# Layer 2's first pass activated by halves of tokens, and a reciprocal issued ahead of its neighbour

## The chip, the cores and the metric

The kernel runs on one core of a Trainium2 chip. The metric is the device time of one execution in microseconds (us): the median of three runs. A core has five engines that run beside each other, each with its own queue worked off in order: TensorE (PE in the profile, with its weight loads as PEld), VectorE (DVE), ScalarE (ACT), GpSimd (POOL) and SyncE (SP), which here only issues DMAs. They wait for each other through semaphores.

## The reference

Attention over 4 batches of 8 heads, 576 tokens, head size 64, with a softmax that keeps only the scores within tau of the maximum, and behind it two feed-forward layers over all 2304 tokens (512 to 2048 to 512). What matters here:

```python
scores = np.where(scores >= thresh, scores, -1000000000.0)
attn = np.exp(scores - np.max(scores, axis=-1, keepdims=True))
attn = attn / (np.sum(attn, axis=-1, keepdims=True) + 1e-09)
x = attn @ v                               # then layer 1, another activation
h = x @ w_in                               # layer 2
r = np.maximum(h, 0.0)
out = (s * (r * r) + b) @ w_out
```

## The kernel before

Every piece of work is a task with a priority, the tiles that it reads and writes, and one or more engines that could do it, with an assumed duration for each. A planner (`Sched.run`) plays the tasks through against these durations and writes the instructions out in the order in which it started them; on the chip each engine then follows that fixed order. Until 460 us of its own clock the planner multiplies the duration of each ACT, DVE and POOL task by a factor between 1.0 and 1.1, taken from a random sequence in the order in which the tasks start:

```python
                    if now < DRAW_TO and e in ("act", "dve", "pool"):
                        t.fn = (e, t.fn[1] * (1.0 + SPREAD * rnd.random()), *t.fn[2:])
```

Attention comes first, in 80 tiles of queries (`qtiles`). 64 of them hold two heads, 16 hold one. A tile goes through the scores on PE, the row minimum (L646, DVE), the exponential (L649, ACT), the mask with its sum (L654, DVE), then three small steps on that sum: `un`, a fallback for empty rows (L667 on POOL or L668 on DVE), `rc`, the sum plus 1e-9 (L670 on POOL or L671 on DVE), and the reciprocal of `rc` (L673, DVE). The normalization (L684 POOL, L689 ACT, or DVE) reads both `rc` and `un`, and PE transposes its result (L715) for the product with the values (L773). `un` and `rc` depend on the same sums and not on each other. Both have the same priority, so the one that is added first goes first.

Matmuls of layer 1 (L968, L1001) have a lower priority than attention and fill PE beside it, once their weights are converted; until 200 us of its clock the planner puts in small matmuls on the identity (L1572, "fills") where PE would otherwise have nothing to do. After attention comes the rest of layer 1, then three passes over the tokens in three blocks of 768: pass 0 is layer 1's second half of the hidden units, pass 1 is layer 2's first half, pass 2 (the last) layer 2's second half. In these passes the order of PE's products is fixed: each product task writes "pe order".

One block of a pass is `gemm1`, seven products p in the order 1, 5, 6, 3, 2, 7, 4 (pass 2: 1, 2, 5, 6, 3, 7, 4), each for four tiles j of hidden units and for n = 384 tokens, and then a second product: `gemm2` with six tiles of tokens over eight rows of hidden units in pass 1 (L1467), `gemm2_products` in pass 2 (L1425). A product's 384 columns in PSUM are copied (`copied`, L1193 ACT or L1194 DVE) or added (`joined`, L1197 DVE) into rows of 768 tokens, `even` and `odd`. `even` has both its halves after p = 3 and p = 2, `odd` after p = 7 and p = 4.

In pass 1 `activated` works on a whole row of 768: positive part (L1229), square (L1230), scale and bias (L1231 DVE, L1232 ACT or L1233 POOL), and a split into a high part (L877, ACT) and a low part (L570 POOL or L571 DVE) that the second product reads. In pass 2 `activated_part` does the first three by halves of 384 (L1243, L1246, L1247 to L1249), and for p = 4 it takes the positive part straight from PSUM (L1245), so that product is not copied. PSUM has eight banks. The products p = 1, 6, 7 and 4 of one j add up in one bank, so four banks stay taken until p = 4 has been read out. The copies and additions have priority -2, ahead of the activations at -1.

Of the kernel before, what the change touches and what calls it, by code (L numbers as in the profile page):

```python
# [12 lines left out]
ALU = mybir.AluOpType  # L13
AX = mybir.AxisListType

B, H, S, D = 4, 8, 576, 64
# [51 lines left out]
BT = 768  # L68
# [308 lines left out]
def attention_then_ffn(tc, qk, v, tau, w1, w2, s2, b2, out):  # L377
    nc = tc.nc
    sch = Sched()

    def add(alts, prio, r=(), w=(), group=None, lag=0, after=0.0):
        mems = {k[0] for k in (*r, *w) if isinstance(k, tuple)}
        r = list(r)
        if "late" not in r and mems & {"LG", "MD"}:
            r.append("late")
        if mems & {"PR", "PF"}:
            r.append("final")
        return sch.add(alts, prio, r, w, group, lag, after)
# [9 lines left out]
    ident = lp.tile([128, 128], F32, name="ident")  # L398
    tau_c, cst = lp.tile([128, 1], F32, name="tau"), lp.tile([128, 5], F32, name="cst")
    half, s_c, b_c, part_c, tiny_c = (cst[:, i:i + 1] for i in range(5))  # L400
# [213 lines left out]
    def qtiles(u, blk):  # L614

        n = ctr["tile"]
        ctr["tile"] += 1
        mixed = blk == 4
        turned = mixed and units[u][0] >= SPLIT
        nx = 1 if mixed else 2  # L620
        p, st = P[n % NP], ST[n % NST]
        kp = [("P", n % NP, x) for x in range(4)]
        ks = [("ST", n % NST, x) for x in range(2)]
        ksm = [("SM", n % NST, x) for x in range(2)]
        krc, kun = ("RC", n % NST), ("UN", n % NST)
        nm, nthr, sm, rc, un = (st[:, 2 * j:2 * j + nx] for j in range(5))
        prs = []
        kth = [("thr", n % NST, x) for x in range(2)]

        def thr(xs, pr):  # L630
            a, o = nm[:, xs[0]:xs[-1] + 1], nthr[:, xs[0]:xs[-1] + 1]
            add([("pool", 300, lambda: nc.gpsimd.tensor_scalar(out=o, in0=a, scalar1=tau_c, scalar2=0.0, op0=ALU.add, op1=ALU.add)),
                 ("dve", 122, lambda: nc.vector.tensor_scalar(out=o, in0=a, scalar1=tau_c, scalar2=None, op0=ALU.add))],
                (-1,) + pr, r=[ks[x] for x in xs] + ["tau"], w=[kth[x] for x in xs])

        def head(x):
            pr = prio_a()
            prs.append(pr)
            ke = kp if mixed else kp[2 * x:2 * x + 2]
            g = scores(u, blk, x)  # L640
            kg = ("bank", g)

            def Sv():
                return PS[g.banks[0]][:, :, 0:HS]

            add([("dve", 665, lambda: nc.vector.tensor_reduce(out=nm[:, x:x + 1], in_=Sv(), axis=AX.XY, op=ALU.min))],  # L646
                at(pr, "min"), r=[kg], w=[ks[x]], group=g)
            ev = p[:, x * S:x * S + S].rearrange("p (a c) -> p a c", a=2)
            add([("act", 624, lambda: nc.scalar.activation(out=ev, in_=Sv(), func=AF.Exp, bias=nm[:, x:x + 1], scale=-1.0))],  # L649
                at(pr, "exp"), r=[kg, ks[x]], w=ke, group=g)  # L650
            thr((x,), pr)

            def mask():
                nc.vector.scalar_tensor_tensor(out=ev, in0=Sv(), scalar=nthr[:, x:x + 1],  # L654
                                               in1=ev, op0=ALU.is_le, op1=ALU.mult, accum_out=sm[:, x:x + 1])

            def late_mask():
                add([("dve", 735, mask)], at(pr, "mask"), r=[kg, kth[x]], w=[ksm[x]] + ke, group=g)

            return late_mask  # L660

        for x in range(nx):
            head(x)()
        pr = prs[-1]

        rs = [ksm[x] for x in range(nx)]
        add([("pool", 240, lambda: nc.gpsimd.tensor_scalar(out=un, in0=sm, scalar1=0.5, scalar2=1.0 / S, op0=ALU.is_lt, op1=ALU.mult)),  # L667
             ("dve", 122, lambda: nc.vector.tensor_scalar(out=un, in0=sm, scalar1=half, scalar2=part_c, op0=ALU.is_lt, op1=ALU.mult))],  # L668
            (-1,) + pr, r=rs + ["ident"], w=[kun])
        add([("pool", 195, lambda: nc.gpsimd.tensor_scalar(out=rc, in0=sm, scalar1=1e-9, scalar2=1.0, op0=ALU.add, op1=ALU.mult)),  # L670
             ("dve", 122, lambda: nc.vector.tensor_scalar(out=rc, in0=sm, scalar1=tiny_c, scalar2=None, op0=ALU.add))],  # L671
            (-1,) + pr, r=rs + ["ident"], w=[krc])
        add([("dve", 75, lambda: nc.vector.reciprocal(out=rc, in_=rc))], (-1,) + pr, w=[krc])  # L673

        def norm(x):
            runs = [(0, 128, x * S, x * S, S)]
            if turned:

                runs = [(64, 128, 0, S, 64), (64, 128, 64, 0, 512), (0, 64, 0, 0, S)]

            def scaled(eng):
                def fn():
                    for i, j, a, o, w in runs:
                        eng.tensor_scalar(out=p[i:j, o:o + w], in0=p[i:j, a:a + w], scalar1=rc[i:j, x:x + 1], scalar2=un[i:j, x:x + 1], op0=ALU.mult, op1=ALU.add)  # L684
                return fn

            def scaled_act():
                for i, j, a, o, w in runs:
                    nc.scalar.activation(out=p[i:j, o:o + w], in_=p[i:j, a:a + w], func=AF.Identity, scale=rc[i:j, x:x + 1], bias=un[i:j, x:x + 1])  # L689

            add([("pool", 2170 if turned else 800, scaled(nc.gpsimd)), ("dve", 1050 if turned else 490, scaled(nc.vector), True),
                 ("act", 2060 if turned else 760, scaled_act)],
                at(pr, "norm"), r=[krc, kun], w=kp if mixed else kp[2 * x:2 * x + 2])

        for x in range(nx):
            norm(x)
        for x in range(nx):
            blocks_of_keys(u, pr, p, kp[3 * x], 0 if not x else S + 64, x, mixed, blk)
        if mixed:
            last_keys(u, pr, p, kp[1:3], mixed, blk, kp[:1])  # L700
        else:
            tails.append((p, kp[1:3]))
            if blk % 2:
                two_tails(u, pr, blk)
# [559 lines left out]
    def gemm1(P, T, first):  # L1264
# [17 lines left out]
        for p in P.order:  # L1282
            pe, sp, po = fresh()
            i = P.order.index(p)
            if p == 4:
                P.early = pe[1] - 1
            r = first_ring[i] if first else ring[i % len(ring)]
            for o, u, v in made.get(p, ()):
                add(both_tt(T, o[0], u[0], v[0], ALU.subtract), sp, r=u[1] + v[1], w=o[1])
            split(T, lambda r=r: r(0, T), lambda r=r: r(BT, T), val[p][0], val[p][1], r.keys(0, T), r.keys(BT, T), sp, pairs_of)  # L1290
            for j in range(nj):
                if p == 1:
                    A[j] = Group(ANY if first else ANY8)
                elif p == 5:
                    Bk[j] = Group(ANY8)
                g = A[j] if p in (1, 6, 7, 4) else Bk[j] if p in (5, 3) else Group(ANY8)
                u = P.unit[P.product(p, j)]

                def mm(g=g, u=u, r=r, p=p):
                    o = bank[g.banks[0]][:, 0:n]  # L1300
                    i = 0
                    for k in range(2):
                        ah, al = u(k * 128, 128), u(256 + k * 128, 128)
                        xh, xl = r(k * n, n), r(BT + k * n, n)
                        for a, y in ((ah, xh), (ah, xl), (al, xh)):
                            nc.tensor.matmul(o, a, y, start=(i == 0 and p in (1, 5, 2)), stop=(i == 5), skip_group_check=p not in (1, 5, 2))  # L1306
                            i += 1

                product(pe, 6 * mm_ns(n), mm, u.keys() + r.keys() + ["four"] * (first and p == ORDER[1]), g)
                even, odd = even_b[j], odd_b[j]  # L1310
                row, at_, n_ = {1: (even, 0, 0), 5: (odd, n, 0), 6: (even, n, 0), 3: (even, n, 1), 7: (odd, n, 1), 2: (even, 0, 1), 4: (odd, 0, 0)}[p]
                whole = P.last and p == 4
                if not whole:
                    (joined if n_ else copied)(g, n, lambda row=row, at_=at_: row(at_, n), row.keys(at_, n), po)
                if P.last:
                    if p in (3, 2, 7, 4):
                        activated_part(at_, n, row, po, g if whole else None)
                elif p == 2:
                    shaped(T, even, G_b[2 * j], po)
                elif p == 4:  # L1320
                    shaped(T, odd, G_b[2 * j + 1], po)
# [326 lines left out]
```

## Time and profile before

| | us |
|---|---|
| median of three runs | 1054.3 (1054.04 to 1054.55) |
| profiled execution, its own time | 1054.88 |
| span of the profiled execution, first to last instruction | 1053.0 |
| attention with layer 1 beside it | 0 to 450 |
| rest of layer 1 | 450 to 497 |
| pass 0 | 497 to 686 |
| pass 1 (a block's first part 29, its second 33) | 686 to 872 |
| pass 2 and the end (a block's first part 29, its second 30) | 872 to 1053 |

The profiled execution lies 0.6 us above the median. 1.9 us of its time lie outside the span. The granted TensorE clock is at its higher level throughout.

### The profile page before, as it was taken

The page shows a single profiled execution, that of the slowest core. Times are in us where ns is not written, and L with a number is a line of the kernel's source. Part 1 is how long each engine was busy: PE and PEld are TensorE (multiplying, and loading weights), DVE is VectorE, ACT ScalarE, POOL GpSimd, SP SyncE. Part 2 cuts the span into 40 slices and gives each one's busy share as a digit, 9 for nine tenths or more (in the row PEclk, how much of TensorE's full clock was granted, in tenths as well). Part 3 has the DMA queues.
Part 4 walks back from the last instruction along what each step waited for, and adds up shares of the span by engine and source line. Part 5 has one row for each costly group of instructions (what it writes and reads, how often), then busy time and mean ns, then how long its engine had stood idle before and what let it go on. Part 6 is the DMA issues. An engine that isn't in the chain of part 4 may idle for free.

```text
span 1053.0 us, 20177 instructions
## 1 busy us (share of the span) xinstructions
PE 1035.4 (98%) x6810; PEld 935.9 (89%) x6810; DVE 863.4 (82%) x1743; ACT 721.8 (69%) x1390; POOL 497.4 (47%) x745
## 2 busy tenths in 40 slices
PE   9999999999999999999999999999999999999998
PEld 6656877799898988999899999998998989999998
DVE  7997989788788798765896978887798956978887
ACT  7987887889898889844454626367595756647381
POOL 5665765889898988642303211121231322424241
PEclk9999999999999999999999999999999999999999
DMA  5654464565646554599955559795569997445531
GB/s 179 200 163 145 136 179 149 180 204 157 187 154 186 167 173 140 192 346 374 367 159 178 193 204 377 249 309 194 186 248 321 383 376 252 148 133 196 172 100 62
DMA packets 117943, 221.54 MB, mean 210 GB/s; under 512 B 12752, under 2 KB 37072, under 8 KB 117840
## 3 DMA queue, kind: packets, MB, share of 16 engines
q1 hardware_dynamic: 117840, 220.25, 62.9%
q8 instruction: 54, 0.88, 0.4%
q14 instruction: 49, 0.40, 0.1%
HBM read 152.96 MB, written 67.24 MB: 209 GB/s over the span
## 4 chain that ended last, share of the span: by engine, by line
PE 87%; ACT 5%; DVE 4%; issue 1%; POOL 1%; DMA 1%; SPq 0%; DVEq 0%; POOLq 0%; ACTq 0%
PE ps L1306 25%; PE ps L1351 9%; PE ps L1467 9%; PE ps L1425 9%; PE ps L968 8%; PE ps L1001 6%; PE ps L773 5%; PE ps L715 4%; PE ps L601 3%; PE ps L592 2%; PE ps L1049 2%; PE ps L774 2%; ACT pt L707 1%; DVE p L654 1%; ACT p L649 1%
## 5 line engine op out<-in xcount | busy, mean ns | idle before, releaser
L1306 PE MATMUL ps<-pr,lr 128*128 128x384 f32 x816 | 144.5, 334 | 0.8 <-DVE pr L571 0.8
L1306 PEld LDWEIGHTS ps<-pr,lr 128*128 128x128 f32 x816 | 141.7, 188 | 1.1 <-DVE pr L571 1.1
L654 DVE SCALAR_TENSOR_TENSOR p<-ps,stt,p 128x576 f32<-128x576 f32 x144 | 115.6, 811 | 28.3 <-ACT p L649 24.7
L1306 PE MATMUL ps<-lr 128*128 128x384 f32 x672 | 121.4, 334 | 1.4 <-ACT pf L1193 1.4
L646 DVE TENSOR_REDUCE stt<-ps 128x1 f32<-128x576 f32 x144 | 106.3, 750 | 15.4 <-PE ps L592 8.9
L1306 PEld LDWEIGHTS ps<-lr 128*128 128x128 f32 x672 | 116.8, 188 | 2.0 <-ACT pf L1193 1.8
L968 PE MATMUL ps<-xh,lr 128*128 128x320 f32 (+1 forms) x512 | 112.4, 299 | 0.6 <-DVE lf L978 0.6
L649 ACT ACTIVATE p<-ps,stt 128x576 f32<-128x576 f32 x144 | 105.1, 744 | 8.8 <-DVE stt L646 8.1
L571 DVE TENSOR_TENSOR pr<-lg,pr 128x768 fp32r<-128x768 f32 (+1 forms) x80 | 71.2, 909 | 25.4 <-PE ps L1467 12.2
L1193 ACT COPY lg<-ps 128x384 f32<-128x384 f32 (+1 forms) x110 | 53.8, 490 | 54.5 <-PE ps L1306 37.5
L1001 PE MATMUL ps<-g,lr 128*128 128x256 f32 (+1 forms) x600 | 88.3, 297 | 0.2 <-ACT lf L1010 0.2
L689 ACT ACTIVATE p<-p,stt 128x576 f32<-128x576 f32 (+3 forms) x99 | 82.4, 839 | 8.2 <-DVE stt L673 7.4
L968 PEld LDWEIGHTS ps<-xh,lr 128*128 128x128 f32 x512 | 85.0, 188 | 1.9 <-DVE lf L978 1.0
L715 PE MATMUL ps<-ident,p 128*128 128x128 f32 x576 | 81.0, 276 | 3.5 <-ACT pt L707 1.7
L1001 PEld LDWEIGHTS ps<-g,lr 128*128 128x128 f32 x600 | 80.7, 188 | 1.6 <-issue 0.8
L715 PEld LDWEIGHTS ps<-ident,p 128*128 128x128 f32 x576 | 65.5, 140 | 17.6 <-ACT pt L707 4.9
L707 ACT COPY pt<-ps 128x512 f32<-128x512 f32 x140 | 77.9, 589 | 4.7 <-PE ps L715 4.2
L1467 PE MATMUL ps<-lr,pr 128*128 128x512 f32 x324 | 76.5, 389 | 0.0
L968 PE MATMUL ps<-xl,lr 128*128 128x256 f32 (+1 forms) x256 | 75.3, 294 | 0.0
L1467 PEld LDWEIGHTS ps<-lr,pr 128*128 128x128 f32 x324 | 60.8, 188 | 12.5
L773 PE MATMUL ps<-pt,vr 128*64 128x256 f32 (+1 forms) x512 | 69.1, 412 | 0.6 <-DVE lf L978 0.5
L570 POOL TENSOR_TENSOR g<-lf,g 128x256 fp32r<-128x256 f32 (+1 forms) x64 | 54.1, 847 | 31.6 <-ACT g L980 25.2
(159 smaller groups left out, 2475.0 us busy)
## 6 DMA issues: line engine op xcount, KB each, us to landing
lr<-wd SPq DMA_DIRECT2D x178, 256.0 KB, 5.2
wd<-lh SPq DMA_DIRECT2D x102, 256.0 KB, 3.9
lk<-in_w_dram SPq DMA_DIRECT2D x48, 512.0 KB, 4.9
vr<-in_v_dram SPq DMA_DIRECT2D x32, 320.0 KB, 3.5
r<-in_qk_dram SPq DMA_DIRECT2D x32, 288.0 KB, 3.1
lg<-y1T SPq DMA_DIRECT2D x6, 1536.0 KB, 8.7
lk<-in_w_dram SPq DMA_DIRECT2D x32, 256.0 KB, 4.2
wd<-pr SPq DMA_DIRECT2D x28, 256.0 KB, 5.5
```

What stands on the lines that cost most here:

```text
L646: add([("dve", 665, lambda: nc.vector.tensor_reduce(out=nm[:, x:x + 1], in_=Sv(), axis=AX.XY, op=ALU.min))], at(pr, "min"), r=[kg], w=[ks[ ...
L649: add([("act", 624, lambda: nc.scalar.activation(out=ev, in_=Sv(), func=AF.Exp, bias=nm[:, x:x + 1], scale=-1.0))], at(pr, "exp"), r=[kg, ...
L654: nc.vector.scalar_tensor_tensor(out=ev, in0=Sv(), scalar=nthr[:, x:x + 1], in1=ev, op0=ALU.is_le, op1=ALU.mult, accum_out=sm[:, x:x + 1])
L707: add([("act", actp_ns(n), lambda: [nc.scalar.copy(out=a, in_=b) for a, b in zip(dst, src())]), ("dve", dve_ns(n), lambda: [nc.vector.tens ...
L715: nc.tensor.transpose(bank[g.banks[0]][:, j * 128:(j + 1) * 128], p[:, c0 + j * 128:c0 + (j + 1) * 128], ident)
L773: nc.tensor.matmul(o[64 * x:64 * x + 64, 0:n], vr[:, c:c + D], PT[:, x, k, c0:c0 + n], start=(k == 0), stop=False)
L968: nc.tensor.matmul(o, a, x, start=(n == 0), stop=(n == 11))
L1001: nc.tensor.matmul(o, a[:, c], x, start=(f == 0 and n == 0), stop=(f == nf - 1 and n == 2))
L1306: nc.tensor.matmul(o, a, y, start=(i == 0 and p in (1, 5, 2)), stop=(i == 5), skip_group_check=p not in (1, 5, 2))
L1351: nc.tensor.matmul(o, w, x, start=(f == rows[0] and s == 0), stop=(f == rows[-1] and s == 2))
L1425: nc.tensor.matmul(o, a, y, start=(k == 0 and p in (1, 7, 4, 5, 2)), stop=(k == 3 * nj - 1), skip_group_check=p not in (1, 7, 4, 5, 2))
L1467: nc.tensor.matmul(o, a, y, start=(f == rows[0] and s == 0), stop=(f == rows[-1] and s == 2))
```

## The change

In `qtiles` the task `un` is moved behind `rc` and its reciprocal. In `gemm1` the last pass's way of activating is extended to pass 1: `whole` now holds for p = 4 of both passes of layer 2, so the copy of that product goes; the four halves are each activated by `activated_part`, and in pass 1 each half is then split into its high and low part. This split may put the high part on ACT or POOL; the one in `activated` allowed ACT alone.

```diff
         rs = [ksm[x] for x in range(nx)]
-        add([("pool", 240, lambda: nc.gpsimd.tensor_scalar(out=un, in0=sm, ...)),
-             ("dve", 122, lambda: nc.vector.tensor_scalar(out=un, in0=sm, ...))],
-            (-1,) + pr, r=rs + ["ident"], w=[kun])
         add([("pool", 195, lambda: nc.gpsimd.tensor_scalar(out=rc, in0=sm, ...)),
              ("dve", 122, lambda: nc.vector.tensor_scalar(out=rc, in0=sm, ...))],
             (-1,) + pr, r=rs + ["ident"], w=[krc])
         add([("dve", 75, lambda: nc.vector.reciprocal(out=rc, in_=rc))], (-1,) + pr, w=[krc])
+        add([("pool", 240, lambda: nc.gpsimd.tensor_scalar(out=un, in0=sm, ...)),
+             ("dve", 122, lambda: nc.vector.tensor_scalar(out=un, in0=sm, ...))],
+            (-1,) + pr, r=rs + ["ident"], w=[kun])
...
-                whole = P.last and p == 4
+                whole = P.layer == 2 and p == 4
                 if not whole:
                     (joined if n_ else copied)(g, n, lambda row=row, at_=at_: row(at_, n), row.keys(at_, n), po)
-                if P.last:
+                if P.layer == 2:
                     if p in (3, 2, 7, 4):
                         activated_part(at_, n, row, po, g if whole else None)
+                    if not P.last and p in (3, 2, 7, 4):
+                        G = G_b[2 * j + (row is odd)]
+                        split(n, lambda G=G, a=at_: G(a, n), lambda G=G, a=at_: G(BT + a, n), lambda row=row, a=at_: row(a, n), row.keys(at_, n),
+                              G.keys(at_, n), G.keys(BT + at_, n), (-1, po[1]), lambda x: x)
                 elif p == 2:
                     shaped(T, even, G_b[2 * j], po)
                 elif p == 4:
                     shaped(T, odd, G_b[2 * j + 1], po)
```

## Rows read from the trace of the kernel before

**Rows 1.** The page, busy time of each engine, share of the span and instructions.

```profile
PE 1035.4 (98%) x6810; PEld 935.9 (89%) x6810; DVE 863.4 (82%) x1743; ACT 721.8 (69%) x1390; POOL 497.4 (47%) x745
```

**Rows 2.** Stretches: length, busy PE, PEld, DVE, ACT, POOL (instructions), clock, DMA share, GB/s.

```profile
0.00:75.00 75.00, 69.77 (x459) 44.53 (x460) 62.96 (x161) 62.81 (x124) 45.93 (x110) 1.00 0.59 179
75.00:150.00 75.00, 71.86 (x512) 53.21 (x510) 65.22 (x172) 64.92 (x139) 48.77 (x93) 1.00 0.49 149
150.00:450.00 300.00, 296.31 (x2232) 258.64 (x2229) 248.44 (x586) 257.92 (x516) 248.70 (x366) 1.00 0.56 174
...
528.00:686.00 158.00, 158.00 (x913) 158.00 (x912) 133.86 (x201) 73.65 (x117) 26.05 (x27) 1.00 0.67 229
686.00:901.00 215.00, 215.00 (x1109) 198.03 (x1108) 170.53 (x287) 147.88 (x260) 53.97 (x66) 1.00 0.80 281
```

**Rows 3.** Chain that ended last, longest pieces: start, length, what; one block of pass 1.

```profile
715.33 32.68 PE ps L1467 x144
748.01 29.14 PE ps L1306 x168
```

**Rows 4.** Stretches of line L1572 alone, the fills: length, PE busy, PEld busy, clock, DMA.

```profile
0.00:75.00 75.00, 11.79 (x72) 9.31 (x72) 1.00 0.59 179
75.00:150.00 75.00, 5.15 (x36) 4.48 (x36) 1.00 0.49 149
```

**Rows 5.** Chain in the first 150 us: start, length, what; fills, then `un` twice.

```profile
15.45 0.42 PE ps L1572 x2
...
28.50 0.25 POOL stt L667
...
89.90 0.20 DVE stt L668
```

**Rows 6.** Two lines' own answers: duration ns min/median/max, first and last start, forms.

```profile
L667 POOL TENSOR_SCALAR stt<-stt x55: 227/247/608, 9.6 to 435.5; 128x2 f32<-128x2 f32 x45, 128x1 f32<-128x1 f32 x10
L668 DVE TENSOR_SCALAR stt<-stt,cst x25: 256/289/1399, 89.8 to 426.8; 128x2 f32<-128x2 f32 x19, 128x1 f32<-128x1 f32 x6
```

**Rows 7.** Line L673: what DVE idled for before it, in us and times.

```profile
  POOL stt L670: 2.1, 5
```

**Rows 8.** Timeline, the first tile: start, length, engine, line.

```profile
9.58 0.25 POOL L667 TENSOR_SCALAR stt<-stt 128x2 f32<-128x2 f32 x1 [1.18 <-DVE p L654]
...
9.90 0.19 POOL L670 TENSOR_SCALAR stt<-stt 128x2 f32<-128x2 f32 x1
...
10.15 0.16 DVE L673 RECIPROCAL stt<-stt 128x2 f32<-128x2 f32 x1
```

**Rows 9.** Chain from 300 to 450 us: both small steps on DVE, the last `un`.

```profile
325.03 1.34 DVE stt L668
326.37 1.40 DVE stt L671
...
389.08 0.07 DVE stt L668
```

**Rows 10.** Groups on ACT from 686 to 901, by shape: count, busy us, mean ns.

```profile
L1229 ACT ACTIVATE lg<-lg 128x768 f32<-128x768 f32 x18 | 14.9, 841 | 1.3 <-DVE lg L1197 1.2
...
L1243 ACT ACTIVATE lg<-lg 128x384 f32<-128x384 f32 x10 | 5.1, 519 | 3.4 <-DVE lg L1197 3.4
```

**Rows 11.** Timeline, end of a first part in pass 1: second product's start, p = 4's last copy.

```profile
715.17 17.88 PE L1467 MATMUL ps<-lr,pr 128*128 128x512 f32 x78
...
716.99 0.54 DVE L1194 COPY pf<-ps 128x384 f32<-128x384 f32 x1
```

**Rows 12.** Timeline, the same place in pass 2: two positive parts back to back, one from PSUM.

```profile
897.33 0.93 ACT L1243 ACTIVATE pf<-pf 128x384 f32<-128x384 f32 x2
...
900.65 11.55 PE L1425 MATMUL ps<-lr,pr 128*128 128x256 f32 x95
...
901.38 0.48 ACT L1245 ACTIVATE lg<-ps 128x384 f32<-128x384 f32 x1
```

**Rows 13.** Stretch of p = 3, 2, 7, 4 in pass 1's second block, columns as in rows 2.

```profile
760.50:777.20 16.70, 16.70 (x98) 16.69 (x97) 16.67 (x28) 14.05 (x23) 9.50 (x11) 1.00 0.81 298
```

More of the change, by code (lines that the diff above doesn't have):

```diff
@@ L666, in qtiles @@
         rs = [ksm[x] for x in range(nx)]
-        add([("pool", 240, lambda: nc.gpsimd.tensor_scalar(out=un, in0=sm, scalar1=0.5, scalar2=1.0 / S, op0=ALU.is_lt, op1=ALU.mult)),
-             ("dve", 122, lambda: nc.vector.tensor_scalar(out=un, in0=sm, scalar1=half, scalar2=part_c, op0=ALU.is_lt, op1=ALU.mult))],
-            (-1,) + pr, r=rs + ["ident"], w=[kun])
         add([("pool", 195, lambda: nc.gpsimd.tensor_scalar(out=rc, in0=sm, scalar1=1e-9, scalar2=1.0, op0=ALU.add, op1=ALU.mult)),
@@ L673, in qtiles @@
         add([("dve", 75, lambda: nc.vector.reciprocal(out=rc, in_=rc))], (-1,) + pr, w=[krc])
+        add([("pool", 240, lambda: nc.gpsimd.tensor_scalar(out=un, in0=sm, scalar1=0.5, scalar2=1.0 / S, op0=ALU.is_lt, op1=ALU.mult)),
+             ("dve", 122, lambda: nc.vector.tensor_scalar(out=un, in0=sm, scalar1=half, scalar2=part_c, op0=ALU.is_lt, op1=ALU.mult))],
+            (-1,) + pr, r=rs + ["ident"], w=[kun])
         def norm(x):
```

## The prediction, made before the changed kernel was run

> **What bounds the kernel now.** I read the page's busy times first: PE is busy for 98% of the span [rows 1], so the reader should ask where the other 2% lie and what of the busy time is not work. The stretches answer the first question. From 528 to 901 us, which is most of pass 0, all of pass 1 and the first part of pass 2, PE is busy for the whole of both stretches (158.00 of 158.00 and 215.00 of 215.00) at the full granted clock [rows 2]. The idle time is in front: 5.23 us in the first 75 us, 3.14 in the next, and 300 - 296.31 = 3.69 in the 300 us behind them [rows 2]. The second question is answered by the fills, 72 in the first stretch and 36 in the second [rows 4], work that nobody reads. Two stand for 0.42 us on the chain [rows 5], so 0.21 each: 15.1 and 7.6 us. In the first 150 us PE thus loses 5.2 + 3.1 + 15.1 + 7.6 = 31 us, because attention, whose tiles go from DVE to ACT and back, doesn't hand it work fast enough; DVE and ACT are busy there for 63 to 65 of 75 us each [rows 2]. After 150 us PE always has layer 1's matmuls at hand, so its total work from there on is fixed, and the time can fall only by what is idle.
>
> **The change, pass 1.** Its three blocks are two pieces of the chain each: 168 matmuls in 29.14 us and 144 in 32.68 us [rows 3], without a gap [rows 2]. The change removes no matmul. So the gain here is nothing, and only a loss is possible. What it does beside PE: each of 24 rows (3 blocks, 4 tiles j, `even` and `odd`) has a positive part, a square, a scaling and two split steps of 768; each becomes two of 384. On ACT a positive part of 768 is 841 ns, of 384 it is 519 [rows 10], but two back to back take 0.93 us [rows 12], so 0.09 more per row and step. For positive part, square and high part: 24 x 3 x 0.09 = 6.5 us more in 215 us, in which ACT is busy for 148 [rows 2]. Away go 12 copies, at 0.54 us for the one shown [rows 11], 6.5 us on ACT and DVE together. Scaling and low part on DVE or POOL have no row for the same tile in both shapes in one stretch; I bound each of the 48 extra pieces by nothing and by the same 0.09, at most 4.3 us, and take it as covered, since DVE is idle for 44 of the 215 us and POOL for 161 [rows 2]. All of this is beside PE.
>
> What can reach PE is when PSUM comes free. The second product wants six banks. Four are free as it begins; the fifth is wanted after four times three matmuls of 32.68 / 144 = 0.227 us, so 2.72 us after its start, the sixth at 3.40. Before, p = 4's last copy began 1.82 us after that start [rows 11], but these copies stand ahead of all activations on ACT, or go to DVE. After the change the positive part from PSUM is on ACT alone, at the activations' own priority, behind the halves of p = 3, 2 and 7. Who waits for it are the fifth and sixth bank's matmuls, and with them everything on PE, whose order is fixed; behind it on ACT are only its own square and split, wanted later still. Pass 2 has this form: there the second positive part from PSUM starts at 901.38, 0.73 us after the second product's start at 900.65, and takes 0.48 [rows 12]. So it ends 1.21 us in, and 3.40 - 1.21 = 2.2 us are left. Pass 1 has four more halves in an unbroken row than pass 2 (p = 2 comes just before p = 7), 4 x 0.93 = 3.7 us of ACT, against 16.70 - 14.05 = 2.65 us that ACT is idle in such a stretch [rows 13]. The overhang of 1.1 us fits into the 2.2. I take nothing, and keep 3.7 - 2.2 = 1.5 us for each of three blocks as the upper bound. The low parts of `odd` are wanted only after 24 x 3 x 0.227 = 16.3 us.
>
> **The change, attention.** A tile on POOL shows the order: `un` 0.25 us, `rc` at 9.90, the reciprocal at 10.15 [rows 8]. With `rc` first the reciprocal could start up to 9.90 - 9.58 = 0.32 us sooner, and `un`, 247 ns in the median [rows 6], then runs beside it. This pays only where the reciprocal waits for `rc`, not for DVE's own turn: DVE idled for that 5 times in 80, 2.1 us in all [rows 7]. On the chain `un` stands nine times, first with 0.25 us and last with 0.07 [rows 5, 9], 6.1 us together; some of these are stretched pieces on DVE like the one of 1.34 us, where the shortest `un` takes 0.26 [rows 6, 9]. Two of the nine, 0.25 and 0.20, lie before 150 us [rows 5]. In the 300 us behind, no gain can be larger than the 3.69 idle there [rows 2]. So the direct gain lies between nothing and 0.45 + 3.69 = 4.1 us. I take 1.0: the 0.45, and for the other seven a third of their unstretched 7 x 0.26 = 1.8, since PE mostly has other work at hand. No DMA is issued by the moved step; behind it on DVE is the next tile's minimum or mask, on POOL the normalization, which needs `un` as well as the reciprocal.
>
> For the stretched pieces the trace shows one more thing: in the tile at 325 us both small steps on DVE are long, 1.34 and 1.40 us, one after the other, so the wait can sit on either [rows 9]. Where it goes over from `un` to `rc`, the reciprocal starts no sooner, and only the two pieces on POOL pay, 0.25 us for the one shown [rows 5]: 0.5 us in all, 1053.8. That is a rival below. The Trainium skill (SBUF — State Buffer, section "Who interferes with whom") says that a VectorE instruction in a two-port mode and a GpSimd instruction exclude each other for a whole instruction, and that the order of issue decides who waits. By that rule the exchange only hands the wait on; the trace agrees as far as both lines stretch.
>
> The larger effect is none of these. The planner draws a random factor for each ACT, DVE and POOL task in the order of their starts, so exchanging two tasks in the first tile shifts every later draw, and the order of all attention work is made anew. What this costs or gives no row shows. Of the 31 us that PE loses before 150 us, the fills alone differ by 15.1 - 7.6 = 7.5 us between two neighbouring stretches [rows 4], so a new order can cost or give at most about that; I take a tenth of the loss, 3 us, either way, as the typical size (an estimate, from the factor's spread of a tenth).
>
> **The sum.** The profiled execution takes 1054.88 us, of which its span is 1053.0; the median is 0.6 lower. Span 1053.0 - 1.0 - 0 = 1052.0, with the 1.9 around it 1053.9, less 0.6: 1053.3 us.
>
> **The rivals.** First: the new order of attention comes out well, fewer fills before 150 us, and the direct gain with it: 1054.3 - 1.0 - 3 = 1050.3. For it: 31 us are there to be had. Against: DVE and ACT keep the same work, 84 to 87% busy. Second, on the other side: ACT falls behind in pass 1 and holds the fifth and sixth bank. It decides from the point where the second positive part from PSUM ends more than 3.4 us after the second product's start; price up to 3 x 1.5 = 4.5 us, with the direct gain 1054.3 + 4.5 - 1.0 = 1057.8. For it: the row of halves is longer than in pass 2. Against: the high part may now go to POOL, idle for 7.2 of 16.7 us [rows 13]. Third: the new order comes out badly: 1054.3 - 1.0 + 3 = 1056.3 and beyond. Fourth: the change doesn't do what it says, because the reciprocal starts at DVE's next turn all the same: 1054.3. For it: only 5 of 80 made DVE idle [rows 7]. Fifth: the wait of a stretched `un` goes over to `rc`: 1053.8, as worked out above.
>
> **How the numbers follow.** A measurement of this kernel tells 0.2%, 2.1 us, from no change. Within it (1052.2 to 1056.4) I put 0.41: 0.20 for my sum, 0.08 for the fourth rival, 0.05 for the fifth, and 0.08 for mild forms of the others. Faster: 0.35, the first rival. Slower: 0.24, half for the banks and half for a bad order. The likeliest own range is 1052.2 to 1056.4. To hold 8 in 10 the range reaches from a little below the first rival, 1049.0, to the bank's full price, 1058.0.
>
> **What would show it.** Right: PE busy for the whole of 528 to 901 again, pieces of 29.1 and 32.7 us in pass 1; ACT there up by a few us; L667 and L668 behind L670 and L671 in each tile; the reciprocal's median distance from the mask shorter; the difference in time all in fills and idle PE before 150 us. Wrong: a wait of L1467 for ACT at the fifth or sixth bank of a block in pass 1, or of L1306 for a late operand; fills that fall or rise by more than 15.

## The result, and the profile after

The changed kernel takes 1062.4 us in the median (1060.33 to 1064.04), against 1054.42 for the kernel before; the ratio is 1.0074 (95% interval 1.0062 to 1.0086). The profiled execution takes 1061.82 us with a span of 1060.0, so 6.9 us more than the one before. The prediction was 1053.3, with a range up to 1058.0.

The first view to open is again the table of stretches, with the same columns as [rows 2]: length, busy PE, PEld, DVE, ACT, POOL, granted clock, DMA.

```profile
0.00:75.00 75.00, 65.52 (x432) 41.83 (x434) 65.04 (x166) 63.76 (x126) 46.15 (x110) 0.98 0.58 180
75.00:150.00 75.00, 74.49 (x535) 55.12 (x531) 66.76 (x178) 65.18 (x139) 48.33 (x90) 1.00 0.49 150
150.00:450.00 300.00, 297.06 (x2233) 259.77 (x2230) 247.74 (x593) 260.18 (x524) 246.02 (x354) 1.00 0.58 182
528.00:686.00 158.00, 158.00 (x914) 158.00 (x912) 137.01 (x209) 74.76 (x117) 38.10 (x26) 1.00 0.75 248
686.00:901.00 215.00, 206.91 (x1042) 187.26 (x1042) 156.24 (x289) 138.72 (x303) 53.42 (x69) 0.99 0.72 252
```

The stretch that had no idle time, 686 to 901, now has 8.09 us of it. The waits of PE in the changed kernel (engine and line, what it waited for, us, times, longest) give it one name:

```profile
PE ps L1471 <- ACT lg L1245: 8.1, 6, 2.3
```

L1471 is the second product of pass 1 (L1467 before), L1245 the positive part read from PSUM. Six waits in three blocks are the fifth and the sixth bank of each block. The timeline at the first block shows both:

```profile
710.78 2.92 PE L1471 MATMUL ps<-lr,pr 128*128 128x512 f32 x12
715.35 0.47 ACT L1245 ACTIVATE lg<-ps 128x384 f32<-128x384 f32 x1
715.87 0.98 PE L1471 MATMUL ps<-lr,pr 128*128 128x512 f32 x3 [2.16 <-ACT lg L1245]
717.74 0.47 ACT L1245 ACTIVATE lg<-ps 128x384 f32<-128x384 f32 x1
718.26 4.07 PE L1471 MATMUL ps<-lr,pr 128*128 128x512 f32 x10 [1.42 <-ACT lg L1245]
```

Twelve matmuls run in the four free banks, then PE waits. The first bank is read out by 715.82, 5.04 us after the second product's start, where 2.72 were allowed; the second by 718.21, at 7.43 us, where 3.40 were. Each time PE goes on 0.05 us later. Before, the last of four copies had begun 1.82 us after that start [rows 11].

The stall costs more than its idle time. Stretches of 2 us behind it, same columns:

```profile
718.00:720.00 2.00, 1.74 (x6) 1.36 (x7) 1.60 (x3) 1.93 (x6) 1.07 (x2) 0.74 0.43 80
720.00:722.00 2.00, 2.00 (x6) 1.63 (x5) 1.52 (x4) 2.00 (x5) 0.00 (x0) 0.50 0.92 242
722.00:724.00 2.00, 2.00 (x9) 1.60 (x9) 2.00 (x6) 0.61 (x2) 0.00 (x0) 0.90 0.63 242
```

Behind these two waits PE's granted clock falls to its lower level, 0.50 (1.2 GHz), and rises again while PE is busy throughout. By the column that is 2 x (0.26 + 0.50 + 0.10) = 1.7 us of lost work, behind a wait that was over.

By the starts of the products in the trace, pass 1's three second products take 38.51, 35.83 and 35.19 us instead of 32.68 each [rows 3], 11.5 us more; the first products still take 29.15. In front, pass 0's first second product starts at 523.59 instead of 527.97 us, 4.4 us sooner. 11.5 - 4.4 = 7.1, which is the difference of the two executions to 0.2 us. In the stretches up to 450 us PE idles for 9.99 + 2.94 us instead of 8.4 + 3.7 [rows 2], but there are 86 fills instead of 108, and PE is busy with them for 14.03 us instead of 11.79 + 5.15 [rows 4], 2.9 us less (PE, PEld, clock, DMA):

```profile
0.00:150.00 150.00, 14.03 (x86) 11.04 (x86) 0.99 0.54 165
```

From 450 to 530 us it idles 0.6 us instead of 2.3. These three make 2.9 - 0.9 + 1.7 = 3.7 of the 4.4 us; the rest isn't split up here. The clock took something back in front, too. The first row is from this profile, the second from that of the exchange alone, which is told below:

```profile
62.50:75.00 12.50, 10.38 (x68) 6.33 (x66) 12.04 (x32) 11.66 (x24) 8.29 (x18) 0.86 0.50 161
62.50:75.00 12.50, 9.10 (x69) 5.51 (x65) 11.70 (x35) 11.83 (x26) 8.38 (x18) 1.00 0.48 160
```

So the change is two effects of opposite sign.

### The profile page after: what moved, and what is told of

Its sections match the earlier page's. It is cut to its first block, busy times and chain, and to the rows that moved or that the text cites. A ratio compares the mean times of both kernels' runs of the same rounds, so it can differ in the third digit from the quotient of the medians.

```text
span 1060.0 us, 20272 instructions
## 1 busy us (share of the span) xinstructions
PE 1035.2 (98%) x6788; PEld 934.3 (88%) x6788; DVE 862.4 (81%) x1787; ACT 726.1 (68%) x1462; POOL 509.0 (48%) x737
## 4 chain that ended last, share of the span: by engine, by line
PE 72%; ACT 9%; DVE 6%; POOL 3%; DMA 2%; issue 2%; DVEq 0%; ACTq 0%; POOLq 0%
PE ps L1306 19%; PE ps L1355 9%; PE ps L1429 9%; PE ps L968 7%; PE ps L1471 6%; PE ps L1001 6%; PE ps L773 4%; PE ps L715 4%; PE ps L601 3%; PE ps L592 2%; PE ps L1049 2%; ACT lf L1246 2%; PE ps L774 1%; ACT lg L1248 1%; DVE p L654 1%
## 5 line engine op out<-in xcount | busy, mean ns | idle before, releaser
L571 DVE TENSOR_TENSOR pr<-lg,pr 128x384 fp32r<-128x384 f32 (+1 forms) x95 | 74.5, 802 | 33.2 <-ACT pr L877 29.1
L1193 ACT COPY lg<-ps 128x384 f32<-128x384 f32 (+1 forms) x104 | 50.9, 492 | 59.6 <-PE ps L1306 32.9
L1471 PE MATMUL ps<-lr,pr 128*128 128x512 f32 x324 | 79.9, 398 | 8.1 <-ACT lg L1245 8.1
L1471 PEld LDWEIGHTS ps<-lr,pr 128*128 128x128 f32 x324 | 61.5, 191 | 23.3 <-ACT lg L1245 10.7
```

Of the source, the lines that this page charges most:

```text
L1471: nc.tensor.matmul(o, a, y, start=(f == rows[0] and s == 0), stop=(f == rows[-1] and s == 2))
```

## The experiments

Every run is timed against the kernel before on the same chip; ratios have their 95% interval.

### The two parts apart

The first kernel has only the halves (`gemm1` as changed, `qtiles` as before), the second only the exchange.

> Pass 1 by halves, attention as before. Theory A, read from the two traces: the change is two separate effects that add up. Pass 1's three second products, each waiting for p = 4's positive part to leave a PSUM bank, cost 38.5 + 35.8 + 35.2 - 3 x 32.7 = 11.4 us, and the new order of attention gives 4.4 us back (the first second-product of pass 0 starts at 523.6 instead of 528.0). Then this kernel takes 1054.4 + 11.4 = 1065.8 us, with the attention's part of the trace ending at 528 as before. Rival B: the loss in pass 1 comes from the earlier start (weights converted or fetched too late for it); then this kernel stands below 1061.

Measured: 1062.55 us, ratio 1.0070 (1.0052 to 1.0088).

> The reciprocal's exchange alone, pass 1 as before. Theory A: 1054.4 - 4.4 = 1050.0 us, passes 0 to 2 without idle PE. Rival B: an earlier start only runs into late weights, so a wait appears behind 528 us and the time is 1053 or more.

Measured: 1050.53 us, ratio 0.9963 (0.9951 to 0.9975).

The signs are as theory A says, and rival B falls: the halves alone lose, with the old start. The size of the first does not fit. Its second products take 36.90, 34.68 and 34.65 us, 8.2 more in all and not 11.4, and its line of waits reads

```profile
PE ps L1471 <- ACT lg L1245: 4.8, 5, 2.0
```

So -3.9 and +8.2 do not add up to the measured +8.0; 3.7 us are missing. Most of it lies in pass 1: there the second positive part from PSUM starts 6.96, 5.91 and 5.29 us after the second product in the whole change, and 5.65, 4.76 and 4.74 with the halves alone, 3.0 us less in sum. The planner's order of pass 1 differs between the two; what in it makes ACT later was not taken further. A smaller piece is in front: pass 0's first second product starts at 523.59 us in the whole change and at 522.75 with the exchange alone, where the clock did not fall.

### Is it the bank?

Two ways to free the bank early. One copies p = 4 out as before and activates the copy; the other keeps the reading from PSUM but gives it the copies' priority. Both have attention as before, and their edits are shown against the halves alone.

```diff
-                whole = P.layer == 2 and p == 4
+                whole = P.last and p == 4
```

> As the kernel with halves alone, but in pass 1 the product p = 4 is copied out of PSUM at the copies' priority as before, and its half activated from the copy. Theory A (a bank is held): the wait of the second product goes, 1054.4 us within 1.5. Rival C (ACT simply has too much to do in these 17 us, and what the second product lacks is the activated operands): a wait of the same size stays under another name, 1062 or more. Small part: 12 copies of 0.48 us more on ACT.

Measured: 1055.68 us, ratio 1.0009 (1.0000 to 1.0019).

```diff
+        early = pr          # before pr = (-1, pr[1])
...
-            add([("act", ..., func=AF.Relu))], pr, r=[("bank", g)], w=kh, group=g)
+            add([("act", ..., func=AF.Relu))], early if first else pr, r=[("bank", g)], w=kh, group=g)
```

> As the kernel with halves alone, but in pass 1 the positive part read from PSUM has the copies' priority, ahead of the other activations. Theory A: the wait goes, since the bank is freed as early as by a copy, though by ACT alone: 1054.4 us, at most 1 us more for each block where the fifth or sixth bank still waits behind a running instruction, so 1054 to 1057. Rival C: 1062 or more.

Measured: 1054.19 us, ratio 0.9993 (0.9983 to 1.0002). Its stretch of pass 1 is as full as before:

```profile
686.00:901.00 215.00, 215.00 (x1109) 197.98 (x1108) 175.64 (x323) 150.55 (x327) 55.13 (x71) 1.00 0.79 280
```

Rival C falls. The same halves cost nothing once the bank is read out first; the 8.2 us come from the wait for the bank, 4.8 of them as idle time. With the copy, 1.5 us stay, and under another name: two of the first products take 30.13 and 29.64 us; 0.7 us of it is a wait for a low part of their operand on DVE (L571), 0.2 us one for an addition on DVE (L1197).

### Why ACT is late, and what else is

The scaling is the longest single step that ACT carries in pass 1, some 0.7 us for a half, so one kernel bars it from ACT there; everything else is the halves alone.

```diff
-             ("act", ..., func=AF.Identity, scale=s_c, bias=b_c)),
-             ("pool", ...)], pr, r=kc + ["sb"], w=kh)
+             ("act", ...), ("pool", ...)][::2 if first else 1], pr, r=kc + ["sb"], w=kh)
```

> Pass 1 by halves, attention as before, the positive part from PSUM at the activations' priority as in the change; the one difference is that pass 1's scaling may go to DVE or POOL only. Theory G: the bank is late because ACT carries 26 of the 48 scalings at 0.6 to 0.7 us, a term that the prediction left on DVE and POOL; taking 8 or 9 of them per block off ACT frees some 5 us, the second positive part from PSUM ends before 3.4 us after the second product's start, and the time is 1054.4 to 1056. Rival C: ACT is late without the scalings too, or DVE now holds up the low parts; 1060 or more.

Measured: 1061.77 us, ratio 1.0064 (1.0047 to 1.0081). The time is nearly that of the halves alone, and yet the wait at the bank is gone: all three second products take 32.68 us. PE's longest wait in pass 1 is now

```profile
PE ps L1306 <- DVE lr L571: 4.1, 2, 3.6
```

and the first block's first product takes 35.71 us instead of 29.15. DVE's and PE's timeline there:

```profile
712.59 0.55 DVE L571 TENSOR_TENSOR pr<-lg,pr 128x384 fp32r<-128x384 f32 x1
713.06 0.47 DVE L1247 TENSOR_SCALAR lg<-lf,cst 128x384 f32<-128x384 f32 x1
713.45 0.95 DVE L571 TENSOR_TENSOR lr<-lf,lr 128x768 fp32r<-128x768 f32 x1
...
714.46 1.97 PE L1306 MATMUL ps<-lr 128*128 128x384 f32 x5 [3.59 <-DVE lr L571]
```

`lr<-lf,lr` is the low part of the operand of p = 4. DVE makes low parts and scalings of halves ahead of it, because activations have priority -1 and operands 0. Nearly half of those 6.6 us are again the clock: it stands at 0.50 from 714 to 720.

```profile
714.00:716.00 2.00, 1.54 (x5) 1.54 (x6) 2.00 (x5) 1.72 (x5) 0.00 (x0) 0.50 0.30 114
716.00:718.00 2.00, 2.00 (x8) 2.00 (x7) 2.00 (x5) 1.66 (x4) 0.00 (x0) 0.50 0.00 0
718.00:720.00 2.00, 2.00 (x8) 2.00 (x7) 2.00 (x4) 1.43 (x3) 0.00 (x0) 0.50 0.00 0
```

Theory G is right on the cause of the bank's wait and wrong on the time. The next kernel keeps the scaling off ACT and puts the operands of p = 7 and p = 4 ahead of the activations:

```diff
             pe, sp, po = fresh()
+            sp = (-1.5, sp[1]) if P.n == 1 and p in (7, 4) else sp
```

> Pass 1 by halves, attention as before, pass 1's scaling on DVE or POOL only, and the operands of p = 7 and p = 4 ahead of the activations. Theory H: the 6.6 us that the first block's first product took longer with the scaling off ACT were the late operand; 1054.4 to 1057. Rival: DVE is simply full and the wait moves on, 1060 or more.

Measured: 1055.92 us, ratio 1.0012 (1.0003 to 1.0022). The late operand was the loss; what stays is 1.44 us in the third block's first product, 1.2 us of it waiting for an addition on DVE (L1197).

### The whole change, mended

Three kernels have the exchange and the halves together: with the positive part from PSUM first, with the scaling off ACT, and with both the positive part and the operands first.

> The whole change, but with the positive part from PSUM at the copies' priority in pass 1. Theory A (bank held): the loss in pass 1 is gone and the new order of attention stays, 1050.5 us within 1.5, pass 1's three second products at 32.7 us each. Rival F: the wait that was larger in the whole change (11.4 us) than with the halves alone (8.1) has another source in the earlier start; then this stands at 1053 or more.

Measured: 1055.83 us, ratio 1.0013 (1.0002 to 1.0023). All second products take 32.68 us, but two first products take 32.53 and 30.64:

```profile
PE ps L1308 <- DVE lr L571: 3.1, 1, 3.1
```

> The whole change with pass 1's scaling on DVE or POOL only. Theory G with the new order of attention: 1050.5 us within 1.5. Rival F: as with the positive part put first (1055.8), another wait comes up in pass 1 in this order, an operand of the first product made late by DVE; then 1053 to 1057.

Measured: 1053.86 us, ratio 0.9995 (0.9986 to 1.0005); one first product takes 31.84 us, for the same operand. In both, rival F is right. In their profiles the clock falls in front as well, so pass 0's first second product starts at 526.09 and 524.41 us instead of 522.75, with the same 86 fills. The first 75 us of the first of them:

```profile
0.00:75.00 75.00, 63.95 (x411) 40.70 (x412) 62.00 (x160) 61.69 (x122) 43.62 (x105) 0.95 0.58 174
```

> The whole change; in pass 1 the positive part from PSUM has the copies' priority and the operands of p = 7 and p = 4 go ahead of the activations. Theory H (pass 1 loses because the halves' chains are begun inside the first product and push back whatever PE needs next: the bank's release or the operand): both are protected, pass 1 is without a wait, 1050.5 us within 1. Rival: a third place waits, 1053 or more.

Measured: 1050.02 us, ratio 0.9955 (0.9942 to 0.9969). Its pass 1 has no wait at all:

```profile
681.00:895.00 214.00, 214.00 (x1102) 197.04 (x1101) 168.16 (x308) 147.87 (x320) 61.47 (x77) 1.00 0.77 268
```

It beats both kernels, but by the exchange: the exchange alone has 1050.53. The halves, with both places protected, bring nothing that these runs can tell from zero.

### Where the gain in front comes from

One kernel keeps the plan of the kernel before, instruction for instruction, and only issues `un` behind `rc` (both on POOL) or behind the reciprocal (both on DVE):

```diff
     order = sch.run()
+    for tu, tr, tq in trios:
+        if tu.fn[0] == tr.fn[0]:
+            order.remove(tu)
+            order.insert(order.index(tq if tu.fn[0] == "dve" else tr) + 1, tu)
```

> The kernel before with its plan kept, instruction for instruction; only where a tile's two small steps stand on the same engine, the step un is put behind rc (on POOL) or behind the reciprocal (on DVE). Theory D (the 3.9 us of the exchange come from the earlier reciprocal itself): 1050.5 to 1053. Theory E (they come from the new order that the planner writes, since every later random factor is shifted): 1054.4 within 1 us, with the fills at 108.

Measured: 1054.45 us, ratio 1.0004 (0.9995 to 1.0013). To issue `rc` and the reciprocal first is by itself worth nothing. Then the kernel before and the exchange alone, each with another start value of the planner's random sequence:

```diff
-DRAW, SPREAD, DRAW_TO = 0, 0.1, 460000.0
+DRAW, SPREAD, DRAW_TO = 1, 0.1, 460000.0
```

> The kernel before with another random sequence for the planner (start value 1 in place of 0), nothing else. Theory E: the new order alone moves the time by several us, with fills and idle time before 530 us differing by that much; the sign is open, 1049 to 1060. Theory D: 1054.4 within 1 us.

> The exchange alone, with start value 1. Theory D: 3 to 5 us below the kernel before with start value 1. Theory E: its distance from that kernel is as large but may have either sign.

> The kernel before with start value 2 for the planner's random sequence. Theory E (a new order moves the time by several us either way; start value 1 gave +8): anywhere from 1049 to 1064, with the difference in fills and idle PE before 530 us.

> The exchange alone with start value 2. Theory E: 1049 to 1064 again, and its distance from the kernel before with start value 2 has no fixed size: -3.9 with start value 0, -1.7 with 1. A third distance near -4 would speak for an effect of the exchange within the planner.

> The kernel before with start value 3. So far 1054.4, 1062.3 and 1056.5 with start values 0, 1, 2. Theory E: 1050 to 1064, with the difference before 530 us.

> The exchange alone with start value 3. Its distances so far are -3.9, -1.7 and -1.6 us. Theory E (pure chance of the order): the sign is open. Theory J (the planner, which takes the exchange into account, gets a denser order from it): 1 to 4 us below the kernel before with start value 3.

> The kernel before with start value 4. Theory E: anywhere from 1050 to 1064.

> The exchange alone with start value 4. Distances so far -3.9, -1.7, -1.6 and +0.4 us. Theory E: either sign, within 5 us. Theory J (the planner draws a gain of its own from the exchange): below the kernel before with start value 4, by 1 to 4 us.

| start value | kernel before, us | exchange alone, us | distance | fills, before and exchange |
|---|---|---|---|---|
| 0 | 1054.4 | 1050.5 | -3.9 | 108, 86 |
| 1 | 1062.3 | 1060.6 | -1.7 | 138, 130 |
| 2 | 1056.5 | 1054.9 | -1.6 | 128, 114 |
| 3 | 1060.4 | 1060.7 | +0.3 | 112, 136 |
| 4 | 1054.1 | 1055.2 | +1.1 | 94, 90 |

Theory D falls, and theory E holds in its main point: with the same work, the order alone moves the kernel before between 1054.1 and 1062.3 us. In the fills' own stretches (line L1572, columns as in [rows 4]) the slowest of these orders shows where: 112 fills before 150 us, and 26 more after it, where there were none.

```profile
0.00:150.00 150.00, 20.07 (x112) 15.74 (x112) 0.99 0.51 158
150.00:450.00 300.00, 3.56 (x26) 3.27 (x26) 1.00 0.57 174
```

The fills are not all of it. The kernel before with start value 3 has 112 of them, four more than with 0, and is 6.0 us slower; PE idles there for 12.30 + 7.36 us up to 450 us instead of 12.06 (all engines, columns as in [rows 2]):

```profile
0.00:150.00 150.00, 137.70 (x963) 97.35 (x965) 128.05 (x329) 128.53 (x265) 95.63 (x203) 1.00 0.54 167
150.00:450.00 300.00, 292.64 (x2186) 252.51 (x2185) 251.41 (x602) 260.70 (x526) 247.74 (x354) 1.00 0.57 180
```

The distances have both signs and a mean of -1.2 us; five pairs do not settle whether the planner draws a small gain of its own from the exchange (theory J). The -3.9 of this change is, as far as five orders tell, mostly the luck of one of them.

## Why the prediction was wrong

*Where PE idles, and that pass 1 could only lose:* right. Pass 1 had no gain to give, and the halves with all waits mended stand within half a microsecond of none. Two readings in front were off. The idle time between 450 and 528 us, 2.25 us, was not on the list, and the exchange took most of it. And the fills were priced at 0.21 us each, 22.7 us in all, where the busy column of the same rows has 11.79 + 5.15 = 16.9 [rows 4]; by it PE loses 25 us before 150 us, not 31.

*The bank:* the place, the mechanism and the point of decision were right (fifth and sixth bank, at 2.72 and 3.40 us), and it was named as the second rival; the step that failed is the overhang of 1.1 us that was said to fit into 2.2. By it the second positive part from PSUM ends 1.21 + 1.1 = 2.3 us after the second product's start; in the first block it ended at 7.43. The overhang was sized with 0.93 us for each of four more halves, the time of two steps on ACT, and the scaling was taken as covered by DVE and POOL. Groups on ACT in the changed kernel from 694 to 717.7 us, in the first block and up to the second positive part from PSUM (count, busy us, mean ns):

```profile
L1248 ACT ACTIVATE lg<-lf,cst 128x384 f32<-128x384 f32 x9 | 6.2, 697 | 0.0
L1246 ACT ACTIVATE lf<-lg 128x384 f32<-128x384 f32 x11 | 5.5, 515 | 0.0
L1243 ACT ACTIVATE lg<-lg 128x384 f32<-128x384 f32 x10 | 4.9, 512 | 1.2 <-DVE lg L1197 1.2
L877 ACT CAST pr<-lg 128x384 fp32r<-128x384 f32 x7 | 3.4, 502 | 0.0
L1248 ACT ACTIVATE pf<-lf,cst 128x384 f32<-128x384 f32 x2 | 1.4, 699 | 0.0
...
L877 ACT CAST pr<-pf 128x384 fp32r<-128x384 f32 x2 | 1.0, 494 | 0.0
```

The same place in pass 2 of the kernel before, from which the prediction started, 872 to 901.35 us:

```profile
L1248 ACT ACTIVATE lg<-lf,cst 128x384 f32<-128x384 f32 x2 | 1.4, 706 | 0.0
L1248 ACT ACTIVATE pf<-lf,cst 128x384 f32<-128x384 f32 x2 | 1.3, 702 | 0.0
L877 ACT CAST pr<-lg 128x384 fp32r<-128x384 f32 x2 | 1.0, 519 | 0.3 <-POOL lg L1249 0.3
L877 ACT CAST pr<-lf 128x384 fp32r<-128x384 f32 x2 | 1.0, 500 | 0.0
...
L877 ACT CAST pr<-pf 128x384 fp32r<-128x384 f32 x1 | 0.5, 508 | 0.0
```

The planner put 11 scalings and 9 high parts of halves on ACT ahead of the second positive part, 7.6 + 4.4 = 12.0 us, where pass 2 has 4 and 5, 5.2 us. These 6.8 us more are what the sum left out. POOL, which was to take such work, was busy for 9.06 of the 21.21 us up to the first positive part from PSUM, and ACT for 19.93:

```profile
694.14:715.35 21.21, 19.57 (x109) 18.71 (x108) 19.11 (x32) 19.93 (x45) 9.06 (x13) 1.00 0.52 182
```

A scaling on ACT is also dearer than its neighbours, 697 ns against 512 and 515. The Trainium skill (ScalarE: Activation LUTs, section "What ACT_TABLE_LOAD costs") gives 186 ns + 0.833 ns per element and 93 ns for each operand that is read from a column; with two such operands that is an estimate of 692 ns for 384, and the trace agrees with 697.

*The price of the bank:* 1.5 us a block was the stated upper bound, 3.8 was measured in the whole change (11.5 / 3) and 2.7 with the halves alone. Part of the gap is the clock, 1.7 us behind the first block's wait, which no term stood for.

*A late operand of the first product:* it was named among the signs of a wrong prediction but had no price. It isn't in the changed kernel, where the bank waits first; it came up in four of the mended ones (the copy, the scaling off ACT without and with the exchange, and the exchange with the positive part first), with 0.7, 4.1, 2.4 and 3.1 us of waiting.

*The reciprocal:* 1.0 us was taken, from two pieces on the chain and a third of seven others; it is nothing (1054.45 against 1054.23). The row that said so was there: DVE idled for `rc` 5 times in 80 [rows 7], and the fourth rival rested on it. The time on a chain is no gain where the engine that ends it has other work.

*The fifth rival,* that a stretched wait passes from `un` to `rc`, is right as an observation. One tile in the kernel before, and the same tile with the plan kept:

```profile
291.88 1.17 DVE L668 TENSOR_SCALAR stt<-stt,cst 128x2 f32<-128x2 f32 x1
292.96 0.22 DVE L671 TENSOR_SCALAR stt<-stt,cst 128x2 f32<-128x2 f32 x1
293.21 0.17 DVE L673 RECIPROCAL stt<-stt 128x2 f32<-128x2 f32 x1
...
291.83 1.12 DVE L671 TENSOR_SCALAR stt<-stt,cst 128x2 f32<-128x2 f32 x1
292.99 0.17 DVE L673 RECIPROCAL stt<-stt 128x2 f32<-128x2 f32 x1
293.07 0.27 DVE L668 TENSOR_SCALAR stt<-stt,cst 128x2 f32<-128x2 f32 x1
```

In this tile the step that is issued first is the long one in either order, and the reciprocal starts 1.16 us after it instead of 1.33. What makes the first step wait no run here shows.

*The new order:* 3 us either way as a typical size was too small. Five orders of the kernel before span 8.2 us, and the order drawn here gave -3.9. That the draws shift with any exchange of two tasks was the right reading; it is what the -4.4 us in front are.

*The sum:* +8.2 for the halves in place of nothing, -3.9 for the order and the reciprocal in place of -1.0, and 3.7 us by which the two together are worse than apart.

## What to carry to other kernels

Where a product's result is kept in an accumulation bank, ask how many banks the next product wants at once and what stands ahead of the read-out on the engine that does it; reading a bank out must not queue behind work that is wanted later. Work begun sooner on an engine that isn't the bound pushes back what the bound needs next, so count every instruction of the step on the engine that a planner may choose, not on the one you hope for. And where instruction order comes from a planner with a random part, an edit's time is known only to the spread between orders; keep the plan fixed, or time several orders, before giving an effect to the edit.

## What the runs showed of the hardware that wasn't expected

Waits of PE of 2.16 and 1.42 us, one soon after the other, were followed by a fall of the granted clock to 0.50 while PE was busy, 1.7 us of lost work; in the kernel with the scaling off ACT the clock stood at 0.50 through three stretches of 2 us behind a wait of 3.6 us. Not every such wait had this effect. Behind 2.26 us in the second block of the changed kernel (first row) and 3.1 us in the kernel with the exchange and the positive part first (second row) the clock stayed at 1.00:

```profile
786.00:788.00 2.00, 2.00 (x11) 1.64 (x10) 1.37 (x4) 2.00 (x6) 0.00 (x0) 1.00 0.50 150
776.00:778.00 2.00, 2.00 (x14) 2.00 (x13) 2.00 (x5) 1.97 (x6) 0.00 (x0) 1.00 0.00 0
```

What decides between the two isn't shown. With the fall, the second product's price was 5.8 us for 3.6 us of waiting in that block; without it, 3.15 us for 2.56 in the next.
